# A state-space mixing kernel: the last unit turned within SBUF, the last quarter's output in two halves, the gate's weights on VectorE, a new order

## The chip, the cores and the metric

The kernel runs on one core of a Trainium2 chip. The metric is the device time of one execution in microseconds (us), the median of several. The engines are TensorE (PE, with its weight loads PEld), VectorE (DVE), ScalarE (ACT), GpSimd (POOL) and SyncE (SP), which here only issues DMAs.

## What is computed

Two state-space models run over the same input u (2048 steps, 512 channels), and a gate mixes their outputs. The reference, cut to its core (`_B_ref` differs from `_A_ref` in how A and C are made and in a factor of 2):

```python
def _A_ref(u, A_re, A_im, B_re, B_im, C_re, C_im, log_dt, Dskip):
    dt = jnp.exp(log_dt)[:, None]
    logdA, dB = dt * (A_re + 1j * A_im), dt * (B_re + 1j * B_im)
    P = jnp.exp(logdA[:, :, None] * l[None, None, :])           # 512 x 128 x 2048
    K = jnp.einsum("dn,dnl,dn->dl", C_re + 1j * C_im, P, dB).real
    y = irfft(rfft(u, 2 * L) * rfft(K, 2 * L))[:L]              # a causal convolution
    return y + u * Dskip

g = sigmoid((x * gate_w).sum(-1, keepdims=True))
return g * a + (1 - g) * b
```

All data are float32.

## The kernel before

The 512 channels are cut into four quarters `q` of 128, and each quarter into two **units** of 64, so there are eight units `v`. For a unit the kernel first makes its **tables** (`tables`, `chunk`): eight chunks of 16 channels of one model. POOL builds angles and magnitudes (L584, L593, L604, L612), ACT takes sines and cosines into PSUM (L624, L626), DVE multiplies (L632 to L647), and PE contracts the 128 modes (L663) to the convolution's kernel K. `put` (L707, copies in L719) is the first half of a Fourier transform of it, written to a tile F. The inputs u go through the same transform (`stage1_u`, `stage2_u`) into HBM (`ud`).

Then `stage2(v)` works in eight **groups** `mg`. For each, `forward` (L730) ends the transform of K on PE, DVE multiplies by the input's transform (L802, L805, tiles z), PE does the first half of the inverse (L814, L815), ACT copies the result from PSUM to a tile `st` (L818; there are two such tiles), and SP writes it to the HBM tensor `wt` (L821). The group's tile has 128 rows p = (x, s), x of 4 and s of 32, with four row numbers m of 128 values each.

`final(q)` (L836 to L859) needs these values **turned**: rows (m, x), columns (s, value). The turn happens on the way through HBM: `wt` is written in one order and read back in the other, in four blocks `bk` of 8 s, two reads of 512 KB each (one per unit). PE multiplies a block by the weights (L847): 16 matmuls of 128 columns, which the trace shows as 32 instructions; ACT or DVE copies it to an st tile (L858, L856), and SP stores 256 KB to the output (L859). The weights are the inverse transform's, times g in `wg`, and times 1 - g in `wb`, so that the gate costs nothing more on PE. For the last quarter the four blocks are read into four places (`LAST`).

`gate` makes g: PE sums u times `gate_w` (L876), ACT takes the sigmoid, and POOL makes `wg` (L894) and `wb` (L906) in 32 instructions of 128x128.

The order of all this is set before the kernel is built. Each piece of work is an `op` with an engine, a cost, a due time, and the tiles that it reads and writes. `Plan.run` goes through time as it would pass, and on each engine takes the ready piece with the earliest due time. The due times come from the tables of numbers at the head of the file (TO, LAG, FSP, FL, YSP and so on). EV, EU, ZU, OE and GE choose DVE or ACT for the copies. FILL puts matmuls of no effect (L310) in front of some pieces of PE, one unit being 128 columns. On each engine instructions then run in that order, waiting for one another by semaphores.

Of the kernel before, what the change touches and what calls it, by code (L numbers as in the profile page):

```python
# [11 lines left out]
ALU = mybir.AluOpType  # L12

P = 128
L = 2048
D = 512
NJ, NS = 32, 64
NV = 8
EV = (15, 196, 44, 189, 18, 211, 128, 80)
EU = (39, 99, 127, 30)  # L20
NQ = 4
NCH = 128
NCK = 16
CHUNKS = ((1, 0), (1, 1), (0, 0), (0, 1), (1, 2), (1, 3), (0, 2), (0, 3))
LAST = ("Fp", "AB", "AB", "F")
ZU = (255, 128, 184, 234)
GE = 3
OE = (4, 13, 8, 0)
PI = math.pi
TWO32 = 4294967296.0  # L30
MAGIC = 12582912.0
# [13 lines left out]

CAPS = {"kg": KG, "kh": KH, "s1": 2, "fb": 4, "pm": 1}
BW = 290e3
PEF = 1.06
IFETCH = 4.0
LAT = {'T': 0.25, 'A': 0.16, 'V': 0.13, 'G': 0.1, 'D': 1.8}  # L50
SWITCH = 0.262
TO = (-1.889, 0.005, 0.391, 0.421, 0.602, 0.774, 1.661, 5.265)
LAG = (0.678, 0.121, -0.62, 0.477, 0.872, 1.512, 4.278, 7.364)
FSP = (-2.006, -2.192, 1.959, 1.655, 1.811, 2.589, -0.871, -0.729)
FL = (4.107, 10.09, -2.659, -0.278)
YSP = (1.66, 2.513, -1.787, -16.884)
UX = (0, 3)
UDS = (-6.649, -1.57, -4.295, -1.364)
USP = (1.939, 0.559, 5.396, 1.718)
GD = 0.534  # L60
GSP = 4.331
GWD = 8.799
TWD = 1.835
UAHEAD = 2.271
UPRE = 0.377
FPRE = 4.586
AN = (-6.143, -2.474, -9.225, -1.896, -0.5, -6.495, -2.674, -9.466)
PT = (-3.361, -3.152, -3.024, -1.108)
PC = (-3.555, -6.036, -6.485, 5.539)
PO = (2.108, 0.737, 1.469, -2.402, -0.966, 1.236, -0.901, -3.632)  # L70
AO = (-0.424, 0.018, 2.018, 4.001, 1.933)
CX = 0.17
CA = 2.776
CV = 0.604
CK = -0.229
CE = -2.162
CS = -3.748
FW = -1.82


FILL = {1: 1, 3: 9, 4: 1, 5: 14, 18: 9, 37: 1, 41: 2, 67: 1, 90: 1, 145: 1, 150: 7, 154: 14, 191: 2, 197: 3, 199: 10, 220: 5, 269: 6, 304: 26}


def _flat(t):
# [27 lines left out]
class Plan:  # L112
# [44 lines left out]
    def run(self):  # L157
# [15 lines left out]
        while n < len(self.ops):  # L173
            nxt = 1e30
            for e in at:
# [30 lines left out]
                o = best[2]  # L206
                ready[e].pop(best[1])
                if e == "T":
                    if turn in FILL:
                        order.append(self.spare(FILL[turn], min((f, t, i) for t in ("ps", "sd") for f, i in free[t])))  # L210
                    turn += 1
                cost = o.cost
                if o.func and o.func != table:
# [42 lines left out]
def gated_s4_mix(ctx: ExitStack, tc: tile.TileContext, ins: dict, out: bass.AP):  # L256
# [526 lines left out]
    def stage2(v, due, sp):  # L783
        F, q = Ft[v], v // 2
        fw = [done[v, 0, 0]]
        for mg in range(8):
            dm = due + sp * mg / 8
            Z1, Z2, hb, st = Buf("z"), Buf("z"), bank(), Buf("st")
            if mg % 2 == 0:
                U = Buf("U")  # L790
                up = mg // 2
                op(
                    "D", 0.5, dm - UPRE, lambda U=U, up=up: DMA(U.v("p (w n) -> p w n", w=2, n=512), both(ud_t[q, v % 2, up])),
                    r=[ud[q, 2 * up], ud[q, 2 * up + 1]], w=[U], nbytes=524288, after=[fw[max(0, len(fw) - 3)]],
                )
# [22 lines left out]
            op("A", 0.48, dm, lambda hb=hb, st=st: A.copy(st.t, hb.t), r=[hb], w=[st])  # L818
            op(
                "D", 0.5, dm,  # L820
                lambda st=st, mg=mg: DMA(  # L821
                    wt_t[v, 4 * mg : 4 * mg + 4].rearrange("m p c -> p m c"), st.v("p (m c) -> p m c", m=4, c=P)
                ),
                r=[st], w=[(wt[v], ((mg, mg + 1),))], nbytes=262144,
            )

    def final(q, due):

        for bk in range(4):
            dy = due + YSP[q] * bk / 4  # L830
            f, y, o = Buf(LAST[bk] if q == NQ - 1 else "Fp"), bank(), Buf("st")
            fv = lambda f=f: f.v("p (u s k c) -> p u s k c", u=2, s=8, k=2, c=64)
# [10 lines left out]
            def mms(y=y, fv=fv, bk=bk):  # L843
                for a in range(4):
                    for k, w in enumerate((wb.t.rearrange("p (s c) -> p s c", c=64), wg)):
                        for e in range(2):
                            T.matmul(  # L847
                                y.t[64 * e : 64 * e + 64, 128 * a : 128 * a + 128].rearrange("p (u c) -> p u c", u=2),
                                w[:, 8 * bk + 4 * e + a, :],
                                fv()[:, :, 4 * e + a, k],  # L850
                                start=(k == 0), stop=(k == 1),
                            )

            op("T", 1.9, dy, mms, r=[f, wgB], w=[y], hold=[wb], nbytes=64)
            if OE[q] >> bk & 1:
                op("V", 0.61, dy, lambda o=o, y=y: V.tensor_copy(o.t, y.t), r=[y], w=[o])  # L856
            else:
                op("A", 0.48, dy, lambda o=o, y=y: A.copy(o.t, y.t), r=[y], w=[o])  # L858
            op("D", 0.5, dy, lambda o=o, bk=bk: DMA(out[q, bk], o.t), r=[o], nbytes=262144)  # L859

    wb, wdone = Buf("W"), []

    def gate(due):

        gs = Buf("Fp")
        for i in range(4):
            y = bank("pm")
            for q in range(NQ):
# [5 lines left out]
                op(  # L874
                    "T", 0.88, de,
                    lambda t=t, q=q, y=y: T.matmul(  # L876
                        y.t, gw[:, q : q + 1].to_broadcast([P, P]), t.t[:, 0:512], start=(q == 0), stop=(q == NQ - 1)
                    ),
                    r=[t, gwB], w=[y], nbytes=4,
                )  # L880
# [6 lines left out]
        op("A", 1.9, d1, lambda: A.activation(gs.t, gs.t, AF.Sigmoid), w=[gs], func="G")  # L887
        for i in range(4):

            def weigh(i=i):  # L890
                for h in range(2):
                    for s3 in range(2):
                        s0 = 16 * (i // 2) + 8 * s3 + 4 * (i % 2)
                        G.tensor_tensor(  # L894
                            wg[:, s0 : s0 + 4, 32 * h : 32 * h + 32],
                            gs.t[:, 512 * i : 512 * i + 512].rearrange("p (h s a j) -> p h s a j", h=2, s=2, a=4, j=NJ)[:, h, s3],
                            w1i[:, 32 * h : 32 * h + 32].unsqueeze(1).to_broadcast([P, 4, NJ]),
                            ALU.mult,
                        )

            def rest(i=i):
                s0 = 16 * (i // 2) + 4 * (i % 2)
                for h in range(2):
                    for s3 in range(2):
                        cut = lambda t: t[:, s0 + 8 * s3 : s0 + 8 * s3 + 4, 32 * h : 32 * h + 32]
                        G.tensor_tensor(  # L906
                            cut(wb.t.rearrange("p (s c) -> p s c", c=64)),
                            w1i[:, 32 * h : 32 * h + 32].unsqueeze(1).to_broadcast([P, 4, NJ]), cut(wg), ALU.subtract,
                        )
# [151 lines left out]
```

## Time and profile before

| | |
|---|---|
| median of 3 runs | 499.2 us (498.7 to 499.8) |
| the profiled execution | 501.76 us, its span 499.8 us |
| mean granted TensorE clock | 0.983 |
| last instruction of POOL ends | 443.19 us |
| last copy of the last group (L818) | 480.84 to 481.43 us |
| last store issued | 496.8 us |

The profile has a page and views of the trace. "Busy" is the time in which an engine had an instruction running. The chain of waits follows the work that ended last back from the end: at each step to what released it. Views by stage give each engine's busy time between two points of the span. A row such as "0.59 ACT st L818" in the chain is 0.59 us of ACT writing tile st in line 818. All line numbers here are those of the kernel before; in the changed kernel the lines stand 2 or 3 lower up to `stage2`, and further below.

### The profile page before, as it was taken

Reading aid. Unit: us, or ns where it says so; the run is one execution under the profiler, and the core shown is the slowest. Engines: PE = TensorE matmul, PEld = TensorE weight load, DVE = VectorE, ACT = ScalarE, POOL = GpSimd, SP = SyncE. Lnnn points to the kernel's source line nnn. Section 1 sums busy time; section 2 is a strip of 40 time slices with the busy share of each in tenths; the row PEclk is TensorE's granted clock in tenths of the full one; section 3 lists DMA queues with packets and bytes.
Section 4 is the critical chain, followed back from the end, with each engine's and each line's share of the span. In section 5 each row is a group of like instructions: output and inputs, shape, how many; then the busy total and the mean of one; then the engine's idle time right before and its main releaser. Section 6 shows DMA issues by size and latency. Waiting matters only on the chain.

```text
span 499.8 us, 21986 instructions
## 1 busy us (share of the span) xinstructions
PE 441.7 (88%) x9662; PEld 384.2 (77%) x9662; DVE 399.7 (80%) x569; ACT 387.3 (77%) x594; POOL 393.9 (79%) x365
## 2 busy tenths in 40 slices
PE   3959978989989899986999988799999899999995
PEld 2658867888667688875888877498888799898965
DVE  5749987998968998998978899959879989792420
ACT  4658969979988889789999889958999976772111
POOL 4494999865999999999799999949999999940000
PEclk9979999999999999997999999899999999999999
DMA  8928663685433355341336667272564145686745
GB/s 271 398 85 249 205 190 118 184 270 145 123 126 108 109 188 169 110 129 64 96 115 209 215 229 193 69 230 69 193 218 164 46 138 159 199 263 221 237 131 203
DMA packets 69439, 85.46 MB, mean 171 GB/s; under 512 B 4704, under 2 KB 50144, under 8 KB 69088
## 3 DMA queue, kind: packets, MB, share of 16 engines
q1 hardware_dynamic: 69344, 84.06, 52.7%
q8 instruction: 76, 1.25, 1.0%
q14 instruction: 19, 0.16, 0.1%
HBM read 50.49 MB, written 33.59 MB: 168 GB/s over the span
## 4 chain that ended last, share of the span: by engine, by line
PE 32%; ACT 21%; DVE 20%; POOL 12%; issue 9%; DMA 4%; SPq 1%; DVEq 0%; ACTq 0%; POOLq 0%
PE ps L730 7%; PE ps L663 5%; PE ps L814 5%; PE ps L707 5%; PE ps L815 5%; ACT sd L624 4%; DVE QD L632 4%; POOL E L612 3%; DVE E L642 3%; PE ps L847 3%; ACT x L625 3%; DVE z L805 3%; ACT sd L626 2%; POOL E L604 2%; POOL x L584 2%
## 5 line engine op out<-in xcount | busy, mean ns | idle before, releaser
L612 POOL TENSOR_TENSOR E<-AB 128x1024 f32<-128x1024 f32 x64 | 125.5, 1962 | 0.1
L814 PE MATMUL ps<-z,c_t 128*128 128x128 f32 x512 | 103.4, 284 | 6.3 <-DVE z L802 2.8
L815 PE MATMUL ps<-z,c_t 128*128 128x128 f32 x512 | 100.5, 278 | 1.3 <-DVE z L805 0.5
L632 DVE TENSOR_TENSOR QD<-sd,E 128x1024 f32<-128x1024 f32 x64 | 78.0, 1218 | 20.4 <-ACT sd L624 8.3
L814 PEld LDWEIGHTS ps<-z,c_t 128*128 128x128 f32 x512 | 78.4, 193 | 12.0 <-DVE z L802 2.5
L730 PE MATMUL ps<-F,c_g 128*128 128x128 f32 x640 | 83.8, 278 | 2.2 <-DVE F L719 1.2
L624 ACT ACTIVATE sd<-x 128x1024 f32<-128x1024 int32 x64 | 66.0, 1031 | 23.6 <-POOL x L584 12.0
L815 PEld LDWEIGHTS ps<-z,c_t 128*128 128x128 f32 x512 | 78.1, 193 | 3.2 <-DVE z L805 3.2
L730 PEld LDWEIGHTS ps<-F,c_g 128*128 128x128 f32 x640 | 75.9, 189 | 5.5 <-ACT F L719 2.1
L604 POOL TENSOR_TENSOR E<-AB 128x512 f32<-128x512 f32 x64 | 68.7, 1074 | 14.5 <-PE ps L663 10.7
L642 DVE TENSOR_TENSOR E<-sd,E 128x1024 f32<-128x1024 f32 x64 | 77.8, 1215 | 1.0 <-ACT sd L626 1.0
L593 POOL TENSOR_TENSOR x<-pi,c_tm 128x512 int32<-128x512 int32 x64 | 68.4, 1070 | 11.4 <-ACT sd L626 7.5
L663 PE MATMUL ps<-E 128*32 128x64 f32 x2048 | 64.1, 222 | 6.4 <-DVE E L642 3.1
L625 ACT ACTIVATE x<-x 128x1024 f32<-128x1024 int32 x64 | 67.8, 1059 | 1.3
L584 POOL TENSOR_TENSOR x<-gh 128x512 int32<-128x512 int32 x64 | 68.6, 1073 | 0.2
L626 ACT ACTIVATE sd<-x 128x1024 f32<-128x1024 f32 x64 | 66.0, 1031 | 2.3 <-DVE E L642 0.8
L663 PE MATMUL ps<-QD 128*32 128x64 f32 x2048 | 63.4, 219 | 2.0 <-issue 2.0
L802 DVE TENSOR_TENSOR z<-ps,U 128x512 f32<-128x512 f32 x64 | 43.7, 683 | 25.5 <-PE ps L730 24.8
L818 ACT COPY st<-ps 128x512 f32<-128x512 f32 x64 | 37.2, 585 | 32.6 <-PE ps L815 27.4
L663 PEld LDWEIGHTS ps<-E 128*32 128x32 f32 x2048 | 48.3, 109 | 18.3 <-issue 8.3
L663 PEld LDWEIGHTS ps<-QD 128*32 128x32 f32 x2048 | 50.3, 110 | 2.5 <-issue 2.5
L707 PE MATMUL ps<-w,K 64*64 64x64 f32 x2048 | 40.1, 222 | 9.9 <-issue 4.3
(123 smaller groups left out, 779.0 us busy)
## 6 DMA issues: line engine op xcount, KB each, us to landing
U<-ud SPq DMA_DIRECT2D x32, 512.0 KB, 3.8
wt<-st SPq DMA_DIRECT2D x64, 256.0 KB, 2.7
X<-wt SPq DMA_DIRECT2D x26, 512.0 KB, 5.7
ud<-z SPq DMA_DIRECT2D x32, 256.0 KB, 3.4
U<-in_u SPq DMA_DIRECT2D x16, 256.0 KB, 4.9
ud<-z SPq DMA_DIRECT2D x32, 128.0 KB, 3.4
U<-in_uT SPq DMA_DIRECT2D x16, 256.0 KB, 3.6
out<-st SPq DMA_DIRECT2D x16, 256.0 KB, 4.2
```

The source lines that it names most:

```text
L584: G.tensor_tensor(xi()[:, :, 1, :].rearrange("n c (a b) -> n c a b", a=4), t[:, :, 0:4].unsqueeze(3).to_broadcast([P, NCK, 4, 8]), t[:, :, ...
L604: G.tensor_tensor(Ev()[:, :, 0, :].rearrange("n c (a b) -> n c a b", a=4), A1()[:, ca, ::-1].unsqueeze(3).to_broadcast([P, NCK, 4, 8]), BB ...
L612: G.tensor_tensor(Ev()[:, :, 1:3, :].rearrange("n c w t -> n c (w t)"), AA()[:, ca].rearrange("n c w a -> n (c w) a").unsqueeze(3).to_broa ...
L624: op("A", 0.96, e, lambda: A.activation(bv(sn), wv(xi()), AF.Sin, scale=SCL), r=[x], w=[sn], func="S")
L625: op("A", 0.96, e, lambda: A.activation(x.t, x.v(dt=I32), AF.Abs), w=[x])
L626: op("A", 0.96, e, lambda: A.activation(bv(cs), wv(qv(x)), AF.Sin, bias=HALF_PI, scale=-SCL), r=[x], w=[cs], func="S")
L632: lambda: V.tensor_tensor(ev(QD)[:, :, 0::2, :], bv(sn).rearrange("n w c t -> n c w t"), Ev()[:, :, 0::2, :], ALU.mult),
L642: lambda: V.tensor_tensor(Ev()[:, :, 0:2, :], bv(cs)[:, 0].unsqueeze(2).to_broadcast([P, NCK, 2, NJ]), Ev()[:, :, 0:2, :], ALU.mult),
L663: T.matmul(K4[32 * b : 32 * b + 32, gg, :], ev(QD if w else E)[:, c, 2, :], ev(QD if w else E)[:, c, 0:2].rearrange("n h t -> n (h t)"), s ...
L730: T.matmul(b.v("p (k m h e) -> p m k h e", k=2, m=4, h=32, e=2)[:, mm], Gw[:, m, :], Fv(F)[:, :, m, :].rearrange("p (k h) e -> p k h e", k=2),
L814: T.matmul(o, Tw[:, m, 0:128], zv(Z1), start=True, stop=False)
L815: T.matmul(o, Tw[:, m, 64:192], zv(Z2), start=False, stop=True)
```

## The change

Four things change.

1. **The last unit's rows are turned within SBUF.** For unit 7, SP no longer writes a group to `wt`. It issues four DMAs of 64 KB from the st tile straight to a tile `ft` of the F kind: each takes one m, 128 rows of 128 values, and writes them to four rows of 32 x 128 values.
2. **The last quarter's output is made in two halves of channels** (`final_last`). Unit 6's half still comes from `wt`, in two reads of 1 MB, and its multiplications are due before the end; unit 7's half comes from `ft`. The instructions have 64 columns rather than 128. Both halves are copied into one tile `fin` of the AB kind, and four stores of 256 KB end the kernel. `LAST` goes.
3. **The gate's weights are made by DVE**, in eight instructions of 128x512. The gate's sum is written in another order of columns for it, by PE's access pattern.
4. **All tables of numbers are drawn anew**, and with them the order. FILL has 34 places and 156 units, where it had 18 and 113.

```diff
-FILL = {1: 1, 3: 9, 4: 1, 5: 14, 18: 9, 37: 1, 41: 2, ..., 269: 6, 304: 26}
+FILL = {1: 10, 2: 26, 3: 5, 4: 4, 5: 12, 18: 8, 19: 1, ..., 277: 1, 308: 11}
...
             op("A", 0.48, dm, lambda hb=hb, st=st: A.copy(st.t, hb.t), r=[hb], w=[st])
+            if v == NV - 1:
+                op("D", 0.5, dm, lambda st=st, mg=mg: turn(st, mg), r=[st], w=[(ft, ((mg, mg + 1),))], nbytes=262144)
+                continue
...
+    ft = Buf("F")
+
+    def turn(st, mg):
+        s = st.v("p (m c) -> p m c", m=4, c=P)
+        for m in range(4):
+            DMA(ft.t[16 * mg + 4 * m : 16 * mg + 4 * m + 4].rearrange("x (s c) -> x s c", c=P), s[:, m])
...
+    fin = Buf("AB")
+
+    def final_last(u, due):
+
+        q = NQ - 1
+        for b2 in range(2):
+            dy = due + (YSP[q] if u else YS6) * b2 / 2
+            if u:
+                f, r0 = ft, 16 * b2
+            else:
+                f, r0 = Buf("Fp"), 0
+                op(
+                    "D", 0.5, dy - FPRE,
+                    lambda f=f, b2=b2: DMA(
+                        f.v("p (s c) -> p s c", s=16, c=P),
+                        wt_t[2 * q].rearrange("m (x s) c -> (m x) s c", x=4)[:, 16 * b2 : 16 * b2 + 16],
+                    ),
+                    r=[wt[2 * q]], w=[f], nbytes=1048576, after=wdone,
+                )
+            y = bank()
+            for i in range(2):
...
-            op("G", 1.65, d1, weigh, r=[gs, w1iB], w=[(wgB, ((i, i + 1),))])
-            op("G", 1.65, d1, rest, r=[(wgB, ((i, i + 1),)), w1iB], w=[(wgB, ((i + 4, i + 5),))], hold=[wb])
+            op(
+                "V", 0.6, d1, lambda wv=wv, g4=g4, w4=w4: V.tensor_tensor(wv(wg), g4(), w4(w1i), ALU.mult),
+                r=[gs, w1iB], w=[(wgB, ((i, i + 1),))],
+            )
+            op(
+                "V", 0.6, d1,
+                lambda wv=wv, w4=w4: V.tensor_tensor(
+                    wv(wb.t.rearrange("p (s c) -> p s c", c=64)), w4(w1i), wv(wg), ALU.subtract
+                ),
+                r=[(wgB, ((i, i + 1),)), w1iB], w=[(wgB, ((i + 4, i + 5),))], hold=[wb],
+            )
...
-        if v % 2:
+        if v == NV - 2:
+            final_last(0, v + 2 + FL6)
+        elif v == NV - 1:
+            final_last(1, v + 1 + LAG[v] + FSP[v] + FL[v // 2])
+        elif v % 2:
             final(v // 2, v + 1 + LAG[v] + FSP[v] + FL[v // 2])
```

Where this moves instructions, in the rows of the built programs. First the end of SP's row before: the last unit's writes, the four blocks' reads for unit 7, and the stores.

```order
L821 DMA wt<-st_85 128x4x128
L821 DMA wt<-st_86 128x4x128
L836 DMA F_66<-wt 128x1024
L836 DMA AB_68<-wt 128x1024
L836 DMA AB_69<-wt 128x1024
L836 DMA X<-wt 128x1024
L859 DMA out<-st_85 128x512
L859 DMA out<-st_86 128x512
```

The same place in the changed kernel: F_66 is `ft`, and X holds a half of unit 6's rows.

```order
L887 DMA X<-wt 128x2048
L838 DMA F_66<-st_85 4x32x128 x4
L838 DMA F_66<-st_86 4x32x128 x4
L796 DMA U_84<-ud 128x2x512
L838 DMA F_66<-st_85 4x32x128 x4
L838 DMA F_66<-st_86 4x32x128 x4
L887 DMA X<-wt 128x2048
L838 DMA F_66<-st_85 4x32x128 x4
L838 DMA F_66<-st_86 4x32x128 x4
L838 DMA F_66<-st_85 4x32x128 x4
L838 DMA F_66<-st_86 4x32x128 x4
L911 DMA out<-AB_68 128x512 x4
```

Nothing is read back after the last group; the second read of unit 6 stands between the turns of groups 3 and 4. Next, PE's row behind the last group, before: seven filler instructions (26 units), and then the first of four blocks of 128 columns.

```order
L814 MATMUL ps_102<-z_80,c_t 128x128
L815 MATMUL ps_102<-z_81,c_t 128x128
L310 MATMUL sd_104<-c_id 128x512 x6
L310 MATMUL sd_104<-c_id 128x256
L847 MATMUL ps_101<-F_66,X 64x128 x2
L847 MATMUL ps_101<-F_66,wg 64x128 x2
```

In the changed kernel unit 6's last block (from X) stands there first, of which these are the last two rows, then 11 units of filler, and then unit 7's half in 64 columns.

```order
L847 MATMUL ps_103<-X 64x64 x2
L847 MATMUL ps_103<-X,wg 64x64 x2
L313 MATMUL sd_104<-c_id 128x512 x2
L313 MATMUL sd_104<-c_id 128x384
L847 MATMUL ps_102<-F_66,X 64x64 x2
L847 MATMUL ps_102<-F_66,wg 64x64 x2
```

Unit 6's first two blocks stand between groups 3 and 4, and its third behind the forward transforms of groups 6 and 7. Last, the gate's weights on POOL before, between pieces of the tables.

```order
L612 TENSOR_TENSOR E_73<-AB_68 128x16x64
L894 TENSOR_TENSOR wg<-X,w1i 128x4x32 x4
L593 TENSOR_TENSOR x_70<-pi_92,c_tm 128x16x32
L894 TENSOR_TENSOR wg<-X,w1i 128x4x32 x12
L906 TENSOR_TENSOR X<-w1i,wg 128x4x32 x8
L538 TENSOR_TENSOR AB_68<-AB_68,pf_94 128x128x4
```

And on DVE in the changed kernel, a part of the stretch (the first of the eight stands 16 rows earlier, the last two 8 rows later).

```order
L722 COPY F_67<-ps_102 128x8x64
L951 TENSOR_TENSOR wg<-X,w1i 128x2x256 x3
L956 TENSOR_TENSOR X<-w1i,wg 128x2x256 x2
L805 TENSOR_TENSOR z_79<-ps_102,U_83 128x512
L808 SCALAR_TENSOR_TENSOR z_81<-ps_102,sgn,U_83 128x512
L635 TENSOR_TENSOR QD_76<-sd_104,E_74 128x16x2x32
```

The 32 instructions are gone from POOL's row, and eight longer ones stand in DVE's, at three places, between its multiplications.

More of the change, by code (lines that the diff above doesn't have):

```diff
@@ L24 @@
 CHUNKS = ((1, 0), (1, 1), (0, 0), (0, 1), (1, 2), (1, 3), (0, 2), (0, 3))
[L25 to L28, printed above, removed]
+FL6 = 2.05
+YS6 = 10.944
+WLD = 10.708
+ZU = (21, 28, 117, 0)
+GE = 7
+OE = (8, 5, 12, 11)
 PI = math.pi
@@ L51 @@
 SWITCH = 0.262
[L52 to L56, printed above, removed]
-UX = (0, 3)
[L58 to L81, printed above, removed]
+TO = (-1.937, -0.527, 0.478, 0.292, 1.402, 2.649, 4.426, 6.703)
+LAG = (-0.034, 0.003, 1.529, 2.357, 3.069, -0.356, 4.554, 6.529)
+FSP = (-0.536, -4.037, -4.133, 3.935, 2.702, 6.535, 5.507, -1.601)
+FL = (4.978, 9.113, -4.945, -1.706)
+YSP = (-5.399, 4.801, -10.964, -27.186)
+UX = (0, 3)
+UDS = (-7.389, -4.84, -7.816, -6.483)
+USP = (10.14, 4.763, 7.512, -1.42)
+GD = 0.907
+GSP = 6.108
+GWD = -9.204
+TWD = -3.527
+UAHEAD = 1.679
+UPRE = -1.108
+FPRE = -3.981
+AN = (-7.811, -5.834, -16.566, -1.744, 2.107, -7.816, 2.753, -11.664)
+PT = (-6.928, -5.294, -2.341, -4.56)
+PC = (-2.298, -12.566, -6.052, 13.901)
+PO = (1.521, 0.468, 1.291, -2.837, 0.744, 1.58, 1.368, -2.116)
+AO = (-0.154, 0.372, 4.341, 4.977, 0.777)
+CX = 1.126
+CA = 4.048
+CV = 0.343
+CK = -0.805
+CE = -2.398
+CS = -4.731
+FW = -2.957
+FILL = {1: 10, 2: 26, 3: 5, 4: 4, 5: 12, 18: 8, 19: 1, 35: 1, 37: 2, 47: 1, 50: 2, 63: 1, 64: 1, 84: 3, 87: 11, 88: 2, 119: 3, 130: 5, 138: 1, 149: 1, 151: 3, 157: 3, 187: 4, 188: 3, 196: 5, 197: 6, 199: 7, 212: 4, 217: 3, 252: 1, 254: 3, 257: 2, 277: 1, 308: 11}
 def _flat(t):
@@ L208, in run @@
                 if e == "T":
-                    if turn in FILL:
-                        order.append(self.spare(FILL[turn], min((f, t, i) for t in ("ps", "sd") for f, i in free[t])))
+                    at_ = min(((f, t, i) for t in ("ps", "sd") for f, i in free[t]), default=None)
+                    if turn in FILL and at_:
+                        order.append(self.spare(FILL[turn], at_))
                     turn += 1
@@ L825, in stage2, with last @@
             )
+    ft = Buf("F")
[3 more added lines that the diff above has]
+            DMA(ft.t[16 * mg + 4 * m : 16 * mg + 4 * m + 4].rearrange("x (s c) -> x s c", c=P), s[:, m])
+    def last(y, a0, bk, us, fv):
+        n = len(us)
+        for a in range(4):
+            for k, w in enumerate((wb.t.rearrange("p (s c) -> p s c", c=64), wg)):
+                for e in range(2):
+                    o = y.t[64 * e : 64 * e + 64, a0 + 64 * n * a : a0 + 64 * n * a + 64 * n]
+                    T.matmul(
+                        o.rearrange("p (u c) -> p u c", u=n) if n > 1 else o, w[:, 8 * bk + 4 * e + a, :], fv(4 * e + a, k),
+                        start=(k == 0), stop=(k == 1),
+                    )
     def final(q, due):
@@ L841, in final @@
                 )
[L843 to L854, printed above, removed]
+            op("T", 1.9, dy, lambda y=y, bk=bk, fv=fv: last(y, 0, bk, (0, 1), fv), r=[f, wgB], w=[y], hold=[wb], nbytes=64)
             if OE[q] >> bk & 1:
@@ L859, in final @@
             op("D", 0.5, dy, lambda o=o, bk=bk: DMA(out[q, bk], o.t), r=[o], nbytes=262144)
+    fin = Buf("AB")
[17 more added lines that the diff above has]
+            for i in range(2):
+                bk = 2 * b2 + i
+                fv = lambda s, k, f=f, r0=r0 + 8 * i: f.t[:, P * (r0 + s) + 64 * k : P * (r0 + s) + 64 * k + 64]
+                op(
+                    "T", 1.1, dy, lambda y=y, bk=bk, u=u, i=i, fv=fv: last(y, 256 * i, bk, (u,), fv),
+                    r=[f, wgB], w=[(y, ((i, i + 1),))], hold=[wb], nbytes=64,
+                )
+                e = V if (bk if u else OE[q] >> bk) & 1 else A
+                op(
+                    "V" if e is V else "A", 0.35 if e is V else 0.3, dy,
+                    lambda y=y, i=i, bk=bk, u=u, f=V.tensor_copy if e is V else A.copy: f(
+                        fin.v("p (b a u c) -> p b a u c", b=4, a=4, u=2, c=64)[:, bk, :, u],
+                        y.t[:, 256 * i : 256 * i + 256].rearrange("p (a c) -> p a c", a=4),
+                    ),
+                    r=[(y, ((i, i + 1),))], w=[(fin, ((bk, bk + 1), (u, u + 1)))],
+                )
+                if u:
+                    op("D", 0.5, dy, lambda bk=bk: DMA(out[q, bk], fin.t[:, 512 * bk : 512 * bk + 512]), r=[(fin, ((bk, bk + 1), (0, 2)))], nbytes=262144)
     wb, wdone = Buf("W"), []
```

44 lines of the change are left out of this document (19 added, 25 removed).

## The prediction

> **What bounds the kernel now.** I read the page's first part, then the busy time by stage, then the chain that ended last, from its end backwards.
>
> ```profile
> span 499.8 us, 21986 instructions
> PE 441.7 (88%) x9662; PEld 384.2 (77%) x9662; DVE 399.7 (80%) x569; ACT 387.3 (77%) x594; POOL 393.9 (79%) x365
> ```
> ```profile
> core 0: us, PE busy (x) PEld busy (x) DVE busy (x) ACT busy (x) POOL busy (x), PEclk, DMA share, GB/s
> 443.20:461.20 18.00, 16.96 (x393) 15.78 (x390) 9.77 (x13) 7.51 (x13) 0.00 (x0) 1.00 0.66 211
> 461.20:481.50 20.30, 19.98 (x163) 18.49 (x162) 7.82 (x12) 4.69 (x8) 0.00 (x0) 1.00 0.62 206
> 481.50:500.00 18.50, 12.05 (x141) 9.04 (x139) 0.00 (x0) 2.34 (x4) 0.00 (x0) 1.00 0.51 185
> 225.00:265.00 40.00, 35.23 (x518) 30.04 (x518) 34.19 (x51) 38.09 (x69) 36.13 (x53) 0.91 0.29 88
> 34.00:443.20 409.20, 372.89 (x8615) 326.34 (x8616) 363.41 (x498) 354.90 (x531) 373.94 (x337) 0.98 0.52 160
> ```
> No engine of the whole span is full. From 34 to 443.2 us, where the eight tables are made, POOL works 373.9 of 409.2 us and PE 372.9: four engines share that stage, and none can be relieved alone for much. Then POOL is done, PE runs the last unit (98% busy from 461 to 481), and the last 18.5 us are a bare chain:
>
> ```profile
> 468.85 0.91 PE ps L730 x8
> ...
> 474.80 0.91 PE ps L730 x8
> ...
> 480.84 0.59 ACT st L818
> ...
> 481.45 2.28 DMA wt<-st
> ...
> 483.87 3.92 DMA F<-wt
> ...
> 487.92 3.73 PE ps L847 x64
> ...
> 491.71 0.59 ACT st L858
> ...
> 492.33 3.80 DMA out<-st
> ...
> 496.23 0.59 ACT st L858
> ```
> Two groups of the last unit take 5.95 us (474.80 - 468.85). The last group's copy ends at 481.43. Its rows then go to HBM (2.28), come back turned (3.92), are multiplied, copied and stored; the fourth store waits for one of the two st tiles. From 481.43 to the end are 18.4 us, and the last store, from 496.82, takes 3.0 of them. All sums below are against this execution: 501.76 us in all, of which 499.8 is the span. The median of the runs shown is 499.2, so 2.56 goes off at the end.
>
> **1. The turn inside SBUF.** It removes one 2.28 us write and one 3.92 us read from that chain and puts four transfers of 64 KB in their place for each group.
>
> ```profile
> L821 SPq DMA_DIRECT2D wt<-st x64: 359/360/932, 118.6 to 481.4; - x64
> ...
> DMA to landing us min/median/max: 2.3/2.7/6.7
> ```
> ```profile
> DMA  0005999999500000000000600000000000002999
> GB/s 0 0 0 168 299 291 295 291 287 299 160 8 0 0 0 0 0 0 0 0 0 0 131 0 0 0 0 0 0 0 0 0 0 0 0 0 90 295 287 295
> ```
> The first fence is the write's own line: 0.36 us of SP to issue, 2.3 to land at best. The second is the DMA activity from 476 to 481 us, in 40 slices of 0.125 us: one write of 256 KB alone in flight keeps the 16 engines 90% busy or more and moves some 290 GB/s, so it is spread over all of them, and its bytes take 0.9 us of the 2.3.
>
> No row shows a transfer from 128 rows into four. The low end for a group is 0.9 us of moving, as now; the high end is one engine at 18 GB/s (290/16), 14.5 us. I take the low end, since bytes, source tile and piece length (512 B) are those of this row, plus three more issues: 3 x 0.36 + 2.3 = 3.4 us from the last copy to the last landing. SP has room: 1.44 us of issue per group against 2.98 us of PE. The second 1 MB read of unit 6 stands on SP between the turns of groups 3 and 4 and waits for PE's first half; PE does that right after group 3, ahead of the two forward transforms of groups 4 and 5, so nothing is late behind it.
>
> [...]
>
> **2. The last quarter in halves.** Unit 6's half is multiplied before the end; only unit 7's half is left.
>
> ```profile
> 448.66 1.92 PE ps L663 x128
> ...
> 452.79 1.90 PE ps L847 x32
> ...
> 454.69 1.10 PE ps L707 x64
> ```
> ```profile
> L474 DVE TENSOR_TENSOR ps<-ps,pf x4: 432/432/433, 21.4 to 314.6; 128x256 f32<-128x256 f32 x4
> ```
> One output block now is 32 matmul instructions of 128 columns, 1.90 us. A half is 32 of 64 columns. Bounds: half of 1.90, if columns set the pace, and all of it, if the loads of 64 weight columns do. L707 has 64-column instructions with 64 weight columns: 64 in 1.10 us in four corners of the array, 17 ns each; with two halves instead of four corners 34 ns, so 1.1 us a block. The end of the chain becomes 3.4 + 0.1 + 4 x 1.1 + 0.4 (a half block's eviction, by L474) + 3.0 (the last store) = **11.3 us in place of 18.4: -7.1**. The st wait is gone, since a tile of its own holds the output. The filler matmuls there shrink to 11 units, 2.4 us by the row below, less than the 3.4 that PE waits. In front, two of unit 6's blocks stand bare between groups 3 and 4 in the row of PE, **+2.2**; the third lies between forward and inverse, where PE waits for DVE, and the fourth behind the last group, where it waits for the turn: both free.
>
> **3. Gate weights on VectorE.**
>
> ```profile
> L894 POOL TENSOR_TENSOR wg<-X,w1i 128x128 f32<-128x128 f32 x16 | 6.8, 488 | 0.0
> ...
> L906 POOL TENSOR_TENSOR X<-w1i,wg 128x128 f32<-128x128 f32 x16 | 6.8, 480 | 0.0
> ```
> ```profile
> L647 DVE TENSOR_TENSOR E<-sd,E 128x512 f32<-128x512 f32 x64 | 43.7, 683 | 2.9 <-ACT sd L626 2.8
> ```
> ```profile
> L473 DVE TENSOR_TENSOR ps<-p,fi 128x256 f32<-128x256 f32 x4 | 4.8, 1202 | 0.4
> ```
> ```profile
> L473 DVE TENSOR_TENSOR ps<-p,fi x4: 433/880/2616, 20.9 to 314.1; 128x256 f32<-128x256 f32 x4
> ```
> ```profile
> 236.92 2.62 DVE L473 TENSOR_TENSOR ps<-p,fi 128x256 f32<-128x256 f32 x1
> ```
> ```profile
> 235.85 3.39 POOL L906 TENSOR_TENSOR X<-w1i,wg 128x128 f32<-128x128 f32 x8
> ```
> POOL loses 32 instructions, 13.6 us. DVE gains eight of 128x512, 0.683 each: 5.5 us. But they take both inputs from SBUF, which hardly any DVE line does. L473 is one that does: at its best 0.433, like its neighbour L474, once 2.62, and that one ended (239.54) just after a run of POOL instructions (239.24). Its mean of 1.202 is 0.77 over L474. So each gate instruction waits between 0 and 2.2 us for POOL; I take 0.77, and DVE gains 5.5 + 6.2 = 11.7. From 225 to 265 us, where the gate's work stands, DVE has 5.8 us free and ACT only 1.9 (38.09 of 40 busy). So the stage can shorten by at most 1.9, whatever POOL is spared, and grow by 11.7 - 5.8 = 5.9. Behind the gate instructions on DVE are queued the products and the z multiplications, for which PE waits. I take **0**: they stand at three places of DVE's row with other work between, so part of their waits falls where DVE is free.
>
> **4. The new order.**
>
> ```profile
> 480.59 5.75 PE L310 MATMUL sd<-c_id 128*128 128x512 f32 x14
> ```
> That filler is 26 units: 0.22 us a unit. The table now has 156 units, not 113: +9.5 us of PE. The first five places have 32 more (57 for 25), where PE waits for loads; the last place has 15 less. The other 26, 5.7 us, stand in the middle, free in a wait and paid for elsewhere. Seven z copies go from DVE to ACT, and ACT has one table load fewer. The bounds I give the redraw are +5.7 and, by rival D, -10; I take **0**, for nothing in the sums of the engines moves by over 3%.
>
> **Sum:** 501.76 - 7.1 + 2.2 = 496.9 for such an execution, less 2.56: **494 us** for the median. With the redraw and the gate at their bounds 486 to 500.
>
> **Rivals.**
>
> A, four engines for the turn. At 18 GB/s each, 256 KB take 3.6 us, over PE's 2.98 per group. From the first issue, at 461.8, eight groups take 29.1; the 1 MB read in their midst puts 64 KB on each engine, 3.3 us at the 20 GB/s of a read (227 / 0.712 / 16 below); with 1.4 of latency the rows are there at 495.6. The forecast has them at 481.45 + 2.2 + 3.4 = 487.1. The difference is +8.5: **502.5 us**, 496 to 509. For it: the shape of the destination. Against: only that no row shows such a shape slow. Chance 0.20.
>
> ```profile
> DMA packets 238, 0.91 MB, mean 227 GB/s; under 512 B 16, under 2 KB 16, under 8 KB 238
> ...
> q1 hardware_dynamic: 238, 0.91, 71.2%
> ```
> B, on the other side: the four destination rows take no more than one engine gives. Then 64 KB cost 3.3 us at 20 GB/s, 32 of them 105 us, and the rows are there at 568 rather than 487: **575 us**. If transfers that follow one another overlap by half, 523. It decides from 0.90 us per 64 KB: 461.8 + 32 x 0.90 + 1.4 is 492.0, and 4.9 past 487.1 is the whole gain. For it: all bytes of a transfer go to four neighbouring rows. Against: the transfers of a group go to different ones. Chance 0.10. [...]
>
> C, the gate stalls on POOL: DVE becomes the bound of its stage and adds 5.9: **500 us**. It is the 2.62 us row, eight times over. Against: the eight stand at three places, not in one. Chance 0.10.
>
> D, the redraw closes waits in the middle:
>
> ```profile
> POOL E L604 <- PE ps L663: 10.7, 2, 5.5
> ...
> POOL AB L538 <- ACT AB L524: 8.8, 4, 4.7
> ```
> POOL stood idle 19.5 us for these two alone, and without the gate it has 360 us of work in a stage of 409. Half of it won is -10: **484 us**. PE, with 36 us free there, allows that. Chance 0.15.
>
> **How the numbers follow.** The forecast has 0.45. A measurement of this kernel can tell 0.2%, 1 us, from no change. The forecast gives 0.43 faster and 0.02 same; A 0.04 faster, 0.04 same, 0.12 slower; B 0.10 slower; C 0.03, 0.03 and 0.04; D 0.15 faster. Together 0.65 faster, 0.09 same, 0.26 slower. The range 480 to 508 leaves out B and the far ends of the others, under 0.2; the forecast's own is 486 to 500.
>
> **What would show it.** Right: the turn's transfers land in 2 to 3 us each, ACT's copies of the last unit wait for PE and not for a transfer, no HBM read stands after the last copy, and from its end to the span's end are some 11 us. A or B: those copies wait for the turn, and SP's issues stretch behind it. C: the wg lines on DVE have a mean far over 0.7 us. D: POOL ends its tables before 440 us. If POOL ends them past 446, the redraw cost more than I gave it. It would be wrong as a whole if the end of the chain shortens and the tables end as much later.

## The result and the profile after

The changed kernel takes 517.6 us, the median of 4 runs (515.7 to 522.5); the kernel before, beside it, 499.5 us (498.7 to 500.5). The ratio is **1.038, 95% interval 1.030 to 1.046**: slower by 3.8%, where 494 us were forecast. The profiled execution has a span of 514.6 us, 14.8 more than before.

Three stretches of the span, cut where POOL ended (before 443.19, after 439.50), where the last unit's first copy starts and where its last one ends. The columns are the bounds, their length, the busy time of PE, PEld, DVE, ACT and POOL (with instructions), PE's granted clock, and DMA share and GB/s. First the kernel before, then the changed one:

```profile
443.19:461.19 18.00, 16.96 (x393) 15.78 (x390) 9.78 (x13) 7.51 (x12) 0.00 (x0) 1.00 0.66 211
461.19:481.43 20.24, 19.92 (x162) 18.46 (x161) 7.82 (x12) 4.70 (x8) 0.00 (x0) 1.00 0.62 206
481.43:499.80 18.37, 12.12 (x141) 9.09 (x139) 0.00 (x0) 2.34 (x4) 0.00 (x0) 1.00 0.52 187
```
```profile
439.50:458.10 18.60, 18.43 (x374) 17.30 (x374) 10.55 (x15) 7.02 (x10) 0.00 (x0) 1.00 0.29 97
458.10:496.18 38.08, 29.48 (x294) 26.48 (x292) 9.09 (x15) 5.07 (x9) 0.00 (x0) 0.87 0.46 128
496.18:514.60 18.42, 5.78 (x128) 5.67 (x128) 0.85 (x2) 0.75 (x2) 0.00 (x0) 0.72 0.26 79
```
The last unit begins 3.1 us earlier, its eight copies are spread over 38.1 us instead of 20.2 (+17.8), and the end behind them is as long as before, 18.4 us. Together that is the 14.8. So the middle of the kernel lost nothing in this execution, the time is in the last unit alone, and the end that was to shrink to 11.3 did not shrink. PE's granted clock is 0.87 and 0.72 in the last two stretches; in PE's wait ahead of the last half blocks, from 495.44 to 504.89 us, it is 0.67, and 0.65 in these blocks.

The chain of waits of the changed kernel from the first of those copies (start, length, what), cut to what carries it:

```profile
458.10 0.60 ACT st L821
458.71 0.69 SPq L838
...
461.48 2.71 SPq L838
464.19 0.04 issue
464.23 2.04 SPq L838
466.27 0.04 issue
466.31 1.91 SPq L838
468.22 0.04 issue
468.27 7.11 DMA F<-st
475.61 0.59 ACT st L821
...
497.97 6.62 DMA F<-st
504.59 0.30 issue
504.89 5.79 PE ps L847 x128
510.70 0.38 ACT AB L904
511.11 0.42 DVE AB L904
```
L838 is the transfer in `turn`. Before, this chain ran over PE and DVE down to the last copy; now it runs over the turn. An issue on SP was put at 0.36 us and takes up to 2.71 while transfers issued before it are still under way; what holds it up the trace does not show. Of the last 18.4 us, 8.7 lie between the last copy's end and PE's start, where 3.5 were forecast; the four half blocks take 5.79 us, not 4.4; the two evictions 0.85; the last store 3.07.

Who waited for the turn, and the copies' own row on the page (busy, mean ns, then idle time ahead of it and what ended it):

```profile
L838 SPq DMA_DIRECT2D F<-st x32: 546/660/2709, 458.7 to 498.0; - x32
...
  ACT st L821: 28.5, 6
```
```profile
L821 ACT COPY st<-ps 128x512 f32<-128x512 f32 x64 | 37.9, 593 | 56.9 <-DMA F<-st 28.5
```
Before, one of the eight copies of the last unit waited for a transfer, 5.06 us for a write:

```profile
468.63 1.29 ACT L818 COPY st<-ps 128x512 f32<-128x512 f32 x2 [5.06 <-DMA wt<-st]
```
Now six of the eight wait 28.5 us for a turn that has not landed, because there are two st tiles: a group's copy needs the tile of the group before the last one. 45.9 us pass from the first issue (458.7) to the last landing (504.6) for 2 MB, with two HBM reads issued between them.

The DMA activity from 464 to 470 us, in 40 slices of 0.15 us, with almost only the turn in flight:

```profile
DMA  2233233323233233332422632222333232232233
GB/s 85 85 48 24 20 27 24 24 20 27 24 38 34 38 51 61 41 27 34 44 34 41 154 41 41 44 51 51 65 75 58 41 41 38 51 55 58 58 68 75
DMA packets 547, 0.29 MB, mean 48 GB/s; under 512 B 16, under 2 KB 546, under 8 KB 546
```
The share is 0.2 to 0.3 in most slices, as four of 16 engines would give, and SP's queue takes 30.4% of the 16 engines' time; which engines carry a transfer the trace does not show. So far this fits rival A. But A had 72 GB/s at such a share, and here are 48 in the mean and 20 to 40 in many slices. That is what A did not have.

### The profile page after: what moved, and what is told of

Same layout as the page of the kernel before. It is cut to its first block, busy times and chain, and to the rows that moved or that the text cites. A ratio compares the mean times of both kernels' runs of the same rounds, so it can differ in the third digit from the quotient of the medians.

```text
span 514.6 us, 22280 instructions
## 1 busy us (share of the span) xinstructions
PE 449.4 (87%) x9818; PEld 391.8 (76%) x9818; DVE 406.7 (79%) x576; ACT 387.0 (75%) x598; POOL 383.6 (75%) x333
## 4 chain that ended last, share of the span: by engine, by line
PE 34%; DVE 16%; ACT 6%; DMA 5%; issue 5%; SPq 3%; POOL 3%; ACTq 0%; DVEq 0%; POOLq 0%
PE ps L817 7%; PE ps L818 6%; PE ps L733 6%; PE ps L666 5%; DMA F<-st 5%; PE ps L847 4%; SPq L838 3%; PE ps L710 3%; DVE QD L635 3%; DVE E L645 3%; DVE z L808 2%; ACT sd L627 1%; DVE z L805 1%; DVE E L650 1%; ACT x L628 1%
## 5 line engine op out<-in xcount | busy, mean ns | idle before, releaser
L817 PE MATMUL ps<-z,c_t 128*128 128x128 f32 x512 | 105.8, 289 | 11.2 <-DVE z L805 5.1
L818 PE MATMUL ps<-z,c_t 128*128 128x128 f32 x512 | 102.1, 282 | 0.6 <-DVE z L808 0.3
L817 PEld LDWEIGHTS ps<-z,c_t 128*128 128x128 f32 x512 | 80.4, 197 | 18.6 <-issue 7.9
L733 PEld LDWEIGHTS ps<-F,c_g 128*128 128x128 f32 x640 | 78.1, 192 | 10.8 <-ACT st L821 3.9
L818 PEld LDWEIGHTS ps<-z,c_t 128*128 128x128 f32 x512 | 80.1, 197 | 1.4 <-DVE z L808 1.3
L821 ACT COPY st<-ps 128x512 f32<-128x512 f32 x64 | 37.9, 593 | 56.9 <-DMA F<-st 28.5
L808 DVE SCALAR_TENSOR_TENSOR z<-ps,sgn,U 128x512 f32<-128x512 f32 x64 | 47.3, 739 | 0.0
```

Source lines behind the costliest of these rows:

```text
L733: T.matmul(b.v("p (k m h e) -> p m k h e", k=2, m=4, h=32, e=2)[:, mm], Gw[:, m, :], Fv(F)[:, :, m, :].rearrange("p (k h) e -> p k h e", k=2),
```

## The experiments

Four kernels ran together in each batch, beside the kernel before (501.0, 502.1 and 501.3 us in the three batches), so ratios are compared.

### 1. The last unit through HBM again

`e1_hbm`: the turn alone undone; order, halves and the gate on VectorE stay.

```diff
-        for m in range(4):
-            DMA(ft.t[16 * mg + 4 * m : 16 * mg + 4 * m + 4].rearrange("x (s c) -> x s c", c=P), s[:, m])
+        DMA(wt_t[NV - 1, 4 * mg : 4 * mg + 4].rearrange("m p c -> p m c"), s)
...
+            DMA(ft.t[:, 2048 * b : 2048 * b + 2048].rearrange("p (s c) -> p s c", c=P),
+                wt_t[NV - 1].rearrange("m (x s) c -> (m x) s c", x=4)[:, 16 * b : 16 * b + 16])
```


> The changed kernel with one part undone: unit 7's groups go to HBM as before (one write of 256 KB per group) and come back turned in two reads of 1 MB behind the last write; order of all engines otherwise as in the changed kernel. If the turn's transfers are what costs (the engines' theory and the rows' theory alike), ACT's copies of the last unit no longer wait for a transfer, the first copy is still near 458 us, the last 20.2 + 2.2 us later, and from there 2.3 (write) + 4.2 (first MB) + 4.4 (two by two blocks) + 0.4 + 3.0 + 0.5 us to the end: span 495, time 497 us (494 to 500). If instead the new order or the halves are what costs, it stays above 508.

Measured: 503.2 us, ratio 1.005 (1.002 to 1.009), span 501.1. Nearly the whole slowdown goes with the turn. The time was expected at 497 and does not fall below before; experiments 6 to 8 say why.

### 2. Sixteen rows per transfer, and four rows four apart

`e2_rows16` and `e3_apart` change only where the 64 KB of a transfer land; the values then stand in wrong places.

```diff
-            DMA(ft.t[16 * mg + 4 * m : 16 * mg + 4 * m + 4].rearrange("x (s c) -> x s c", c=P), s[:, m])
+            # e2_rows16
+            DMA(ft.t[16 * mg : 16 * mg + 16, 1024 * m : 1024 * m + 1024].rearrange("x (s c) -> x s c", c=P), s[:, m])
+            # e3_apart
+            DMA(ft.t[16 * mg + m : 16 * mg + 16 : 4].rearrange("x (s c) -> x s c", c=P), s[:, m])
```


> The changed kernel, but each of the four transfers of a group writes 16 rows of 8 x 128 values in place of 4 rows of 32 x 128 (the values then lie in wrong places; bytes, source, pieces of 512 B and number of transfers stay). Engines' theory (a transfer into four rows runs on four of the 16 DMA engines): all 16 work, the DMA share in the last unit goes far over 0.25 and the copies wait for PE; time 490 to 497 us. Rows' theory (four neighbouring rows take what one engine gives, whatever the number of engines): four times as many such sets of rows, so also faster, 492 to 500. Issue rival (four times as many transfers, 0.55 to 2.7 us of SP each): unchanged, above 512.

> The changed kernel, but the four rows of a transfer lie four apart (rows m, m+4, m+8, m+12 of the group's 16) in place of side by side; values in wrong places, all else as it was, still four rows a transfer. Engines' theory alone: no change, 512 to 521, the DMA share stays near 0.25. Rows' theory: the stretches at 20 to 60 GB/s go and the turn runs at the four engines' 72 GB/s throughout; eight groups then take some 32 us rather than 46, and the time falls by 8 to 13, to 505 to 510. Issue rival: no change.

Measured: 16 rows 507.9 us, ratio 1.012 (1.005 to 1.019); four rows apart 512.3, ratio 1.022 (1.015 to 1.029). The first was expected at 490 to 500 by both theories, the second at 505 to 510 if the place of the rows counts and at 512 to 521 if it does not. Each takes a part of the 3.8% away and neither all of it, so the activity has to tell more than the time. DMA activity with the turn alone in flight, four rows apart (494 to 499 us), then 16 neighbouring rows (468.5 to 470 us):

```profile
DMA  2331222232222222222232232232222222322222
GB/s 66 70 102 29 57 86 82 70 78 78 86 78 86 82 78 82 82 82 78 74 82 74 66 74 78 74 86 78 74 74 78 78 78 70 78 74 78 78 74 74
DMA packets 750, 0.38 MB, mean 76 GB/s; under 512 B 23, under 2 KB 749, under 8 KB 749
```
```profile
DMA  9999999899997999999999989999899999969699
GB/s 260 178 123 109 137 96 137 68 137 68 109 123 68 150 82 96 123 82 123 96 96 109 137 55 109 109 82 109 68 123 68 109 96 109 96 55 137 55 123 82
DMA packets 353, 0.16 MB, mean 107 GB/s; under 512 B 39, under 2 KB 353, under 8 KB 353
```
Four rows four apart: still a share of 0.2 to 0.3, but a steady 76 GB/s, and the slices at 20 to 40 are gone but for one. Four neighbouring rows (48 GB/s) are thus slower than four rows apart, at the same share. Sixteen rows: a share of 0.9 and more in most slices, yet only 107 GB/s, against 290 for a write of the same tile. So two limits are at work: one that goes by the number of rows and shows in the share, and a second one that goes by which rows are written.

### 3. Sixteen rows eight apart

`e13_rows8` tests the second limit: 16 rows as in `e2_rows16`, but spread, and values again in wrong places. In `e2_rows16` ten of the first eleven slices from 472 to 480 us (0.2 us each) lie between 85 and 143 GB/s. If the place of the rows is what holds these down, 498 to 502 us were expected, and no copy that waits for the turn.

```diff
+            DMA(ft.t[mg : 128 : 8, 1024 * m : 1024 * m + 1024].rearrange("x (s c) -> x s c", c=P), s[:, m])
```


> The turn inside SBUF with four transfers of 64 KB per group into 16 rows that lie eight apart (rows mg, mg + 8, ...), values misplaced. [...] Rival (pieces of 512 B or the number of issues bound it, not the place of the rows): 85 to 140 GB/s again and 506 to 509.

Measured: 504.5 us, ratio 1.005 (1.001 to 1.008). The activity from 467.8 to 469.2 us, when nothing but the turn is in flight:

```profile
DMA  8999999999999999999999999999999999999999
GB/s 235 337 278 366 322 352 322 337 351 293 366 249 249 234 220 205 205 176 190 220 147 205 147 220 190 176 205 161 190 220 147 219 161 190 191 161 205 147 161 147
DMA packets 701, 0.32 MB, mean 227 GB/s; under 512 B 80, under 2 KB 701, under 8 KB 701
```
With the same share, 0.9 and more, the mean rate is 227 GB/s instead of 107; in the second half of either window it is some 180 instead of some 95. The transfers land in a median of 3.1 us rather than 5.0. The place of the rows is a limit of its own. The time, 504.5, is over the 498 to 502 expected: with four issues per group, of 0.60 us in the median, SP reaches unit 6's second read at 476.86 us (470.08 in `e1_hbm`), and PE waits 3.5 us for it. Two copies still wait 2.1 us for the turn, where none was expected to. So with both limits eased the turn is level with the way through HBM (1.005 in experiment 1), and not ahead of it.

How many engines work on a transfer is read from the share alone: 0.2 to 0.3 for four rows, 0.9 and more for 16. Which engines they are no run here shows, nor why the place of the rows counts.

### 4. The turn from GpSimd

`e5_pool` issues the same four transfers by `G.dma_start`. If the four of a group ran side by side from there, at the 100 GB/s that 16 rows had shown, 496 to 501 us were expected.

> The same four transfers per group, issued from GpSimd instead of SyncE. [...] Rival: the queue does not matter, four engines again, or the descriptors cost more on GpSimd: 510 or more.

Measured: 526.3 us, ratio 1.048 (1.043 to 1.053), so worse still, and the rival's number. But it is not the share of four engines again:

```profile
DMA  9396988999968599996799849323102454644586
GB/s 53 30 48 55 85 77 131 336 168 88 61 55 98 131 371 404 319 176 41 56 83 50 34 39 83 19 17 39 11 0 46 78 84 67 72 44 46 67 78 56
DMA packets 1892, 2.85 MB, mean 95 GB/s; under 512 B 1212, under 2 KB 1212, under 8 KB 1761
...
q0 software_dynamic: 1475, 1.24, 50.1%
```
```profile
L838 POOL DMA_DIRECT2D F<-st x32: 687/687/827, 463.0 to 509.9; - x32
...
DMA to landing us min/median/max: 5.2/9.1/13.7
```
The first view is from 470 to 500 us, in slices of 0.75 us. The packets of GpSimd's queue (q0) take 50.1% of the 16 engines' time, where SP's queue took 30.4% in the changed kernel, yet they move 1.24 MB in these 30 us, some 41 GB/s; the slices of 131 to 404 GB/s hold HBM reads beside them. The larger share gained nothing on the same four rows here. That the rows are the reason is not shown, because the queue changes more than the share: none of the 1892 packets in this view has between 512 B and 2 KB, while 530 of the 547 in the changed kernel's view from 464 to 470 us do. Why landing takes 9.1 us in the median, and whether the descriptors cost more on GpSimd, as the rival also had it, was not followed further.

### 5. The gate's engine and the redraw

`e4_hbm_gate_pool` is `e1_hbm` with the gate's eight instructions issued on GpSimd, in the same order. `e7_whole` has the new order and the gate on VectorE, but the last unit through HBM and the last quarter in whole blocks, as before. `e8_before_gate` is the kernel before with only the new `gate`, and `e14_before_gate_pool` that one with the eight on GpSimd.

```diff
-                lambda wv=wv, g4=g4, w4=w4: V.tensor_tensor(wv(wg), g4(), w4(w1i), ALU.mult),
+                lambda wv=wv, g4=g4, w4=w4: G.tensor_tensor(wv(wg), g4(), w4(w1i), ALU.mult),
```


> e1_hbm with the gate's eight weight instructions (128x512) issued on POOL instead of DVE at the same places of the order. If the gate on VectorE costs by its waits for POOL (2.4 us at most in the trace), this is up to 3 us faster than e1_hbm; if POOL's relief is what let the tables end 3.7 us earlier, it is 3 to 9 us slower (POOL has 8 x 1.07 us more). Within 1 us of e1_hbm: the gate's engine does not matter and the rest of the new order made the tables end earlier.

> The changed order and the gate on VectorE, but the last unit through HBM and the last quarter in whole blocks, as before. Theory (the redraw and the gate are worth nothing): 498 to 501, within 0.3% of before. Rival D of the prediction (the redraw closes waits in the middle, seen as the 3.1 us by which the first copy of the last unit came earlier in the changed kernel): 495 to 497.

> The kernel before with the gate's weights on VectorE in eight instructions, nothing else. Theory: no change, 498.5 to 500.5. Rival C (VectorE stalls): 501 to 505. Rival: POOL's 13.6 us freed shorten the middle: 494 to 497.

> The same order as the kernel before with its gate rewritten (525.9 us), but the eight gate instructions issued on GpSimd. Theory (the 24 us of that run come from the order that the old table gives for a changed set of operations, not from VectorE's stalls): 520 to 530 again. Rival C (the gate on VectorE stalls that order): 500 to 505.

Measured: `e4_hbm_gate_pool` 502.6 us, ratio 1.003 (1.000 to 1.007), within 1 us of `e1_hbm`. `e7_whole` 503.8, ratio **1.000** (0.997 to 1.004): redraw and gate together are worth nothing that these runs can tell, as forecast. `e8_before_gate` 525.9, ratio 1.047 (1.041 to 1.052), which none of the three cases named; `e14_before_gate_pool` 520.3, ratio 1.035 (1.030 to 1.041). In the old table's numbers the rewritten gate costs 3.5% with GpSimd doing it: the planner draws another order (DVE's row parts from that of before at about its middle) from numbers fitted to another set of operations. VectorE adds 1.2% there, some 6 us, and under 1 us in the new order. So the redraw is what keeps the rewritten kernel level; it doesn't gain beyond that. Which wait of that other order costs the 3.5% was not followed; one that grew is POOL's for ACT ahead of L538, 19.3 us for 8.8.

### 6. Four reads, and more filler

`e9_hbm4_fill` is `e1_hbm` with four reads of 512 KB and 24 filler units for 11 in front of the last blocks (`FILL[308]`).

> The run through HBM with halves, its two reads of 1 MB cut into four of 512 KB, and 24 units of filler in place of 11 in front of the last four half blocks. Theory (its tail was long because the first half block waited for 1 MB instead of 512 KB, 5.2 us for 3.9, and because the clock had fallen, 1.46 us a half block for 1.08): 1.3 + 1.5 us less than the run with two reads, 499 to 501. Rival: the reads share the same wire and PE's pace there is not set by the clock: within 0.5 us of that run, 502 to 504.

Measured: 503.6 us, ratio 1.002 (0.998 to 1.006) where `e1_hbm` had 1.005; the intervals overlap, and the time is where the rival had it. The trace shows what was meant all the same. PE's first two rows of the half blocks, in `e1_hbm` and here (start, us for four instructions, idle time before):

```profile
491.21 0.48 PE L856 MATMUL ps<-F,X 128*64 128x64 f32 x4 [4.75 <-DMA F<-wt]
491.48 0.43 PE L856 MATMUL ps<-F,wg 128*64 128x64 f32 x4
```
```profile
493.22 0.34 PE L857 MATMUL ps<-F,X 128*64 128x64 f32 x4 [1.03 <-DMA F<-wt]
493.38 0.29 PE L857 MATMUL ps<-F,wg 128*64 128x64 f32 x4
```
With filler up to 1.03 us before the blocks four instructions take 0.29 us; after a bare wait of 4.75 us they take 0.43, half as long again. What goes with it the changed kernel shows: after its bare wait of 9.45 us the granted clock is 0.50 from 504.89 to 508.70 us, where four take 0.45, and 1.00 from 509.0 to 510.5, where they take 0.30. So the rival's reason, that PE's pace there is not set by the clock, does not hold. From the last copy's end to the span's end: 17.6 us in `e1_hbm`, 16.6 here, 18.2 in `e7_whole`. But the first to the last copy's end takes 23.1 us here and 20.4 in `e7_whole`. By these profiles the halves give 1.6 and cost 2.7.

### 7. Unit 6's half blocks behind the last group

`e11_late` mends that: unit 6's four half blocks wait for the last group's multiplications, and stand where filler stood. It has the four reads of `e9_hbm4_fill` and, behind those half blocks, 10 units of filler.

```diff
+        end = () if u else [o for o in pl.ops if o.eng == "T" and o.nbytes == 32]
...
-                f, r0 = Buf("Fp"), 0
+                f, r0 = Buf("AB" if b2 else "Fp"), 0
...
-                    r=[f, wgB], w=[(y, ((i, i + 1),))], hold=[wb], nbytes=64,
+                    r=[f, wgB], w=[(y, ((i, i + 1),))], hold=[wb], nbytes=64, after=end,
...
-        if v == NV - 2:
-            final_last(0, v + 2 + FL6)
-        elif v == NV - 1:
+        if v == NV - 1:
+            final_last(0, v + 1 + FL6)
```


> The run through HBM with four reads, and unit 6's four half blocks all put behind the last group of unit 7, where PE waited for the reads beside 5.4 us of filler (10 units of filler are left). Theory (the halves gained nothing because two to three of unit 6's bare half blocks, 1.0 us each, stood between groups of unit 7 and delayed the last copy by 2.7 us, while the tail shortened by 1.7): from the first to the last copy of the last unit 19.8 us again instead of 22.5, the tail no longer, so 2 to 3 us less than the four-read run: 0.994 to 0.998 of before. Rival: the blocks behind the last group push unit 7's own blocks back: no gain, 1.001 to 1.004.

Measured: 500.3 us, ratio **0.996** (0.992 to 1.000), as expected. ACT's copies of the last unit, the first and the last:

```profile
459.68 0.59 ACT L821 COPY st<-ps 128x512 f32<-128x512 f32 x1 [3.63 <-PE ps L818]
...
479.60 0.59 ACT L821 COPY st<-ps 128x512 f32<-128x512 f32 x1 [1.20 <-PE ps L818]
```
20.5 us with the last copy itself, and 16.4 behind it. This version is the fastest of all, though the interval reaches almost to no change.

### 8. Half of the rows read back early

`e12_late_rows` is `e11_late` with rows 0 to 63 read back ahead of the last two groups' writes.

```diff
+        if mg == 0:
+            DMA(ft.t[0:64], wt_t[NV - 1, 0:16].rearrange("m (x s) c -> (m x) (s c)", x=4))
```


> As the run before it, and rows 0 to 63 (four groups that are written early) are read back ahead of the last two groups' writes, so that 1 MB instead of 2 MB is left behind the last write. Theory: the last read lands some 2 us earlier, 0.990 to 0.996 of before. Rival: the early 1 MB read holds up the last two writes on the same rings by as much, no change against the run before it.

Measured: 505.2 us, ratio 1.006 (1.003 to 1.009). Its rival, and more. The chain's last pieces:

```profile
483.96 6.44 DMA wt<-st
490.52 3.63 DMA F<-wt
494.29 5.32 PE ps L859 x128
```
The last write lands after 6.44 us instead of 2.27: it was issued behind the early read. The first of the reads that are left then lands in 3.63 us, and the four blocks behind it, with the filler long done, run slowly: 5.32 us for 128 instructions, where two stretches of 32 took 1.15 and 1.18 in `e11_late`.

## Why the prediction was wrong

**The step that failed** is part 1, "The low end for a group is 0.9 us of moving, as now ... I take the low end, since bytes, source tile and piece length (512 B) are those of this row". What sets the rate is what is *not* of this row: the destination. One write of 128 rows became four transfers into four rows each. A group's 256 KB took 5.7 us on average (45.9 / 8, with the HBM reads between them) instead of 0.9, over PE's 2.98, and so the turn became the bound of the last unit. Only the destination was changed in experiments 2 and 3, and the ratio went 1.038, 1.022, 1.012, 1.005.

**Rival A**, with four of 16 engines, fits the share and gave 502.5. That a transfer into four rows has four engines no run shows; the runs showed a share of 0.2 to 0.3 with four rows and of 0.9 and more with 16. A was too low in two ways. Its 3.6 us per group are 72 GB/s without a break. With rows apart, where that rate holds (76), the first issue to the last landing still took 37.2 us (462.54 to 499.75) against A's 33.8, and the end behind the landing 10.4 against 7.9: PE began 1.1 after the landing, and the half blocks took 5.3 for 4.4. The rest, from a ratio of 1.022 to 1.038, some 8 us, is the second limit.

**Rival B** had that second limit, priced as if it held alone and always: 575, or 523 with half overlapped. Measured are 1.43 us per 64 KB (45.9 / 32), between its deciding point of 0.90 and its 3.3. A and B were set against each other as cases; their two limits hold together, and the time lies between them.

**SP's room** fell with it: "1.44 us of issue per group" were 0.36 us each from the write's row. At its shortest an issue of the turn took 0.53 to 0.55 us in every layout, 2.2 per group, and in the changed kernel up to 2.7. Nor is it so that "nothing is late behind it": SP came to unit 6's second read at 479.51 us, and PE waited 2.5 us for it.

**The halves** were right in parts: a half block takes 1.08 us where PE has been kept busy (forecast 1.1), the bare blocks in front cost 2.7, the difference between `e9_hbm4_fill` and `e7_whole` (forecast +2.2), and the last store 3.07 (3.0). The part mis-sized is the four half blocks behind the landing, 5.79 us for 4.4: the 11 filler units end at 495.44 us, the rows come at 504.59, and the granted clock is 0.65 in the blocks. The end also has two evictions, 0.85, where the sum has one, 0.4. Without the turn the halves are worth nothing where they stand (1.002 and 1.005 against 1.000 with whole blocks) and 0.4% where the wait covers them.

**The gate** was right: 0.683 + 0.77 = 1.45 us an instruction was forecast, and the eight take 11.2 us, by their means (1.53 + 1.34) / 2 = 1.44 each (busy us, mean ns):

```profile
L951 DVE TENSOR_TENSOR wg<-X,w1i 128x512 f32<-128x512 f32 x4 | 6.0, 1529 | 0.0
L956 DVE TENSOR_TENSOR X<-w1i,wg 128x512 f32<-128x512 f32 x4 | 5.2, 1344 | 0.0
```
That the means agree so closely is partly luck: the 0.77 came from four instructions of 0.43 to 2.62 us, and the eight lie between 0.67 and 2.44. The effect on the time is none that shows in the new order, as forecast. A cost of the size of rival C's 5.9 us, some 6, appears in the order of the old table alone; whether it comes by C's mechanism was not followed.

**The redraw** was right as a sum (1.000), though the reason given, that no engine's sum moves by over 3%, is not one: with the old numbers sums as close as these give +3.5%. So this 0 was right by luck. Rival D is refuted. POOL ended 3.7 us early in the changed kernel and the last unit began 3.1 early, which looks like D and is the sign that the prediction gave for it; but in the ten other runs with the new order the first copy starts between 459.7 and 464.1 us, so 458.1 is no gain to build on.

## What to carry to other kernels

A transfer's price is read from a row with the same shape on *both* sides; if only bytes and source agree, the row prices something else, and the far bound is as good a guess as the near one. Before a transfer replaces another, ask into how many rows it writes and where they lie (here 48 GB/s into four neighbours, 76 into four rows four apart, 107 into 16 neighbours, 227 into 16 rows eight apart), and compare the result with the pace of what produces its source; two limits of one transfer are added to one forecast, not weighed as two. Work that is pulled out of the end pays only where it fills a wait: unit 6's half blocks were no gain between the groups and a small one, 0.4%, in the wait behind them.

## What was not expected of the hardware

- Inside SBUF the rate goes by the rows written: with a share of 0.9 and more of the 16 engines 107 GB/s into 16 neighbouring rows and 227 into 16 rows eight apart, in windows of some 1.4 us; with a share of 0.2 to 0.3, 48 into four neighbours and 76 into four rows four apart.
- An issue on SP took 0.36 us in the median for a write of 256 KB from SBUF to HBM, and 0.56 to 0.66 for 64 KB of the same source within SBUF, with four destination rows or 16.
- Behind a wait of PE of 4.75 us without filler the half blocks took 0.43 us for four instructions; behind filler that left a wait of 1.03 us they took 0.29. In the changed kernel, behind a wait of 9.45 us, they took 0.45 at a granted clock of 0.50, then 0.30 at 1.00.
